# Turning v as float32r by way of a copy in HBM, with two small reorderings, in a fused attention and mixture-of-experts kernel

## The chip, the cores and the metric

The kernel runs on one core of a Trainium2 chip. Its engines are TensorE (PE for matmuls, PEld for the loads of their stationary operand), VectorE (DVE), ScalarE (ACT), GpSimd (POOL) and SyncE (SP), which here issues nearly all of the plain DMAs. Each engine works through its own queue in order, and semaphores order the engines among each other. The metric is the device time of one execution in microseconds (us); less is better.

## The reference

Four batches of q, k and v, each 5056 x 256 in float32, go through an attention over the channels, and its output goes through a mixture of eight experts of which each row takes one:

```python
qn = q / (np.linalg.norm(q, axis=1, keepdims=True) + 1e-06)
kn = k / (np.linalg.norm(k, axis=1, keepdims=True) + 1e-06)
s = kn.transpose(0, 2, 1) @ qn / tau            # 256 x 256 in each batch
a = softmax(s)
x = (v @ a).reshape(20224, 256)
logits = x @ w_gate + modality_bias[modality_id]
e_idx = argmax(logits); gate_w = softmax(logits)[e_idx]
out[rows of e] = gate_w * (np.maximum(x @ w1[e], 0) @ w2[e])   # w1[e]: 256 x 1024, w2[e]: 1024 x 256
```

## The kernel before, in words

**Numbers.** Most products are made of float32r matmuls: an operand is split into a high part (a copy that is rounded to float32r) and a low part (the rest), and three products (high by high, high by low, low by high) are summed in PSUM. The splits are a cast on ScalarE and a subtraction on DVE for each tile.

**Steps.** A batch is cut into ten steps of 512 rows (the last has 448), so there are 40 steps, g = 10 b + s. In a step, `va_pieces(b, s)` has two lists of pieces. The first one loads a tile of v (`load`, the DMA at L559) and turns it: `tr(h)` for the two halves of the channels, each with four transposes of 128 x 128 on TensorE (L576) into the PSUM tile `vtp`, then the high part `vh` on ScalarE (L580) and the low part `vl` on DVE (L582). The second list multiplies by the attention weights: `av(t)` (L596) makes the PSUM tile `xp` of 256 columns of x and 8 columns of logits, and ScalarE copies it out (L600). `route` then finds each row's expert and its place: maximum, exponentials on ScalarE (L611), one-hot rows `oh` (L619), a running count of them on DVE (`tensor_tensor_scan`, L627), three small matmuls `rp` (L632 to L634), positions, and the sum of the exponentials `sm` (L651) with its reciprocal as the gate's weight. Four indirect DMAs then scatter the rows of x to the scratch tensor `xs`, sorted by expert.

**Blocks.** A block is 512 rows (some 384) of one expert. Its rows are loaded from `xs` into a float32r tile `xr`, turned with the float32r identity (`tr_x`, L798) and split; then come eight hidden slices, `m1(j)` (L816, PSUM tag "h") with the activation on ScalarE (L819) and its low part on DVE (L820), and `m2(j)` (L834) into the output tiles; ScalarE scales them (L850) and an indirect DMA scatters them to the output. There are 40 blocks, with weights loaded for each (L758, L762) into buffers three deep and split (L779, L786).

**Next batch.** `kq_pieces(b + 1, s)` loads q and k (L291), squares and sums them (L333, L335) and adds their product to the 256 x 256 Gram matrix of the next batch (L344, L358, L362).

**At a batch's first step** `softmax_pieces(b)` turns the Gram matrix into weights: norms, two softmax pieces, `turn_weights` (transposes into the PSUM tile `atp`, L454, copied to `at` at L458) and `gate_weights`. For batches 1 to 3 the latter calls `gate_columns` for both halves, matmuls of `at` by the gate's matrix (L474) into the PSUM tile `gw`; their result becomes the last eight columns of the weights (L485, L488).

**The order of the work.** In each step the pieces of the block, of softmax, v and `av`, and of q and k are three streams, which `_interleave` mixes in proportion to their lengths; the second stream is written out at L955. From this order of the program a scheduler makes the queue of each engine; it may move a piece's instruction past others that aren't ready by its own model of the times. `order(ins, others)` lays down that an instruction stands behind others on its queue without a semaphore.

**PSUM.** `atp`, `gw`, `vtp` (from step 6 on), `xp`, `rp` and the turned x all have the tag "aux", which has two buffers of one bank each.

Of the kernel before, what the change touches and what calls it, by code (L numbers as in the profile page):

```python
# [34 lines left out]
def kernel(  # L35
# [349 lines left out]
    def softmax_pieces(b):  # L385
# [83 lines left out]
        def gate_columns(m, at):  # L469
            if m == 0:  # L470
                st["gw"] = ps2.tile([P, 512], F32, tag="aux", name=f"gw_{b}")
            gw = st["gw"]
            for jh in range(CH):
                nc.tensor.matmul(  # L474
                    gw[:, m * E : (m + 1) * E], at[:, jh, m * P : (m + 1) * P], small["wg"][:, jh, :],
                    start=(m == 0 and jh == 0), stop=jh == CH - 1, skip_group_check=True,
                )
# [33 lines left out]
    turned = {}  # L511
    routed = {}
# [32 lines left out]

    def va_pieces(b, s):
# [6 lines left out]
        def load():  # L553

            vt = p2.tile([P, TT, C], F32, tag="yo" if g % 2 == 1 and g < first_block else "v", name=f"v_{g}")
            if pp < P:
                z0 = pp // 32 * 32
                nc.vector.memset(vt[z0:], 0.0)
            nc.sync.dma_start(  # L559
                vt[:pp], v[b, t0 : t0 + pp * TT, :].rearrange("(p t) c -> p t c", t=TT)  # L560
            )
# [8 lines left out]
        def tr(h):  # L570
            if early and h == 1:
                tp = ps1.tile([P, 512], F32, tag="y1", name=f"vtp_{g}_{h}")
            else:
                tp = ps2.tile([P, 512], F32, tag="h" if early else "aux", name=f"vtp_{g}_{h}")
            for t in range(TT):
                nc.tensor.matmul(  # L576
                    tp[:, t * P : (t + 1) * P], st["v"][:, t, h * P : (h + 1) * P], ident,
                    is_transpose=True, start=t == 0, stop=True, skip_group_check=True,
                )
            cast[g] = nc.scalar.copy(st["vh"][:, h, :], tp).ins  # L580
            turned.setdefault(g, []).append(("act", cast[g]))
            ins = nc.vector.tensor_tensor(st["vl"][:, h, :], tp, st["vh"][:, h, :].bitcast(F32), ALU.subtract)  # L582
# [19 lines left out]
        def route():  # L602
# [24 lines left out]
            nc.vector.tensor_tensor_scan(rtf, keep, ohf, 0.0, ALU.mult, ALU.add)  # L627
# [23 lines left out]
            nc.vector.tensor_reduce(sm, ex, AX.X, ALU.add)  # L651
# [291 lines left out]
    for g in range(G):  # L943
# [11 lines left out]
        streams.append(soft[:-1] + turn[:1] + soft[-1:] + turn[1:] + va[g][1])  # L955
        if b + 1 < B:
            if b == 0 and s == 1:
                streams.append(list(kq_pieces(1, 2, lambda: routed[1] + turned[2], squares[2])))
            else:
                streams.append([f for i in (PLAN[s] if b == 0 else [s]) for f in kq_pieces(b + 1, i, routed[g - 1] + turned[g] if b == 0 and g > 0 else ())])  # L960
        _interleave(*streams)
# [94 lines left out]
```

## Time and profile before

| what | value |
|---|---|
| time, median of 3 runs | 1252.65 us (1251.12 to 1252.85) |
| the profiled execution's own time | 1244.78 us |
| its span, from the first to the last instruction | 1243.0 us |
| mean granted clock of TensorE | 0.998 |
| matmuls and other TensorE instructions | 8226 |
| moved by DMA | 210.82 MB, 170 GB/s in the mean |

The profile is of one execution. Busy times are given for each engine; a matmul's duration overlaps with its neighbours' since matmuls are pipelined, so the time that it takes from TensorE is read from the starts of two instructions that follow each other. A row of a timeline has the start, the duration, the engine, the line, the operation, the tiles (written <- read) and the count; in brackets stands how long the engine was idle before and what released it. A row of the waits has the engine and line that waited, what it waited for, the total, the number and the longest. The page gives the granted clock and the DMA share in 40 slices of the span, in tenths.

### The profile page before, as it was taken

The numbers are of one execution on the slowest core, as the hardware profiler recorded it, in microseconds if no ns is written. First come the engines' busy times: TensorE is split into PE (matmuls) and PEld (weight loads), VectorE is DVE, ScalarE is ACT, GpSimd is POOL, SyncE is SP. The second block draws the span as 40 slices with busy tenths as digits, with TensorE's granted clock in tenths as the row PEclk, the third lists the DMA queues.
The fourth block names the chain that finished last, engine by engine and source line by source line (L and its number), as shares of the span: only waits on it lengthen the run. The fifth ranks groups of instructions, "written<-read, shape, count | busy, mean of one in ns | idle before, by whom it ended". The sixth has DMA issues, their size and how long they took to land.

```text
span 1243.0 us, 23526 instructions
## 1 busy us (share of the span) xinstructions
PE 1222.3 (98%) x8226; PEld 1113.7 (90%) x8226; DVE 835.2 (67%) x2196; ACT 740.0 (60%) x1519; POOL 356.0 (29%) x344
## 2 busy tenths in 40 slices
PE   9989999999999999999999999999999999999997
PEld 8878898899999999988999999998899999999997
DVE  6689688777677776676766776665565665575552
ACT  6666677766666666665566665565555554545553
POOL 0052333222233333213332333322322233343221
PEclk9999999999999999999999999999999999999999
DMA  8959465455555555545555564434554444443420
GB/s 309 338 167 339 147 212 180 154 176 179 170 175 185 178 178 173 174 155 168 178 173 188 163 182 156 146 111 132 167 168 139 147 157 140 138 146 115 154 98 29
DMA packets 104177, 210.82 MB, mean 170 GB/s; under 512 B 11336, under 2 KB 52808, under 8 KB 104048
## 3 DMA queue, kind: packets, MB, share of 16 engines
q1 hardware_dynamic: 88304, 167.61, 42.7%
q0 software_dynamic: 15744, 41.61, 8.8%
q8 instruction: 66, 1.08, 0.4%
q14 instruction: 63, 0.52, 0.2%
HBM read 167.06 MB, written 43.43 MB: 169 GB/s over the span
## 4 chain that ended last, share of the span: by engine, by line
PE 87%; issue 7%; DMA 2%; DVE 2%; POOL 1%; ACT 1%; POOLq 0%; SPq 0%; DVEq 0%; ACTq 0%
PE y L834 31%; PE hp L816 31%; PE xp L596 10%; PE g L344 4%; PE g L358 4%; PE vtp L576 3%; PE g L362 2%; PE xtp L798 2%; POOL out_dram L515 1%; DMA k<-in_k_dram 1%; PE ns L395 1%; DMA w2r<-in_moe_w_dram 0%; PE gw L474 0%; DVE w1l L786 0%; DMA w1r<-in_moe_w_dram 0%
## 5 line engine op out<-in xcount | busy, mean ns | idle before, releaser
L515 POOL DMA_INDIRECT xs<-x,pi x160 | 178.9, 1118 | 694.4 <-ACT w1h L779 339.9
L834 PE MATMUL y<-w2h,hh 128*128 128x256 f32 x1264 | 355.5, 281 | 0.6 <-ACT yo L850 0.6
L834 PE MATMUL y<-w2l,hh 128*128 128x256 f32 x1264 | 353.4, 280 | 0.0
L834 PE MATMUL y<-w2h,hl 128*128 128x256 f32 x1264 | 352.6, 279 | 0.1
L820 DVE SCALAR_TENSOR_TENSOR hl<-hp,hh 128x512 fp32r<-128x512 f32 (+1 forms) x320 | 217.2, 679 | 65.7 <-ACT hh L819 62.5
L816 PE MATMUL hp<-xh,w1h 128*128 128x512 f32 (+1 forms) x640 | 255.9, 400 | 0.0
L834 PEld LDWEIGHTS y<-w2h,hh 128*128 128x128 f32 x1264 | 238.0, 188 | 14.8 <-ACT yo L850 1.3
L816 PE MATMUL hp<-xl,w1h 128*128 128x512 f32 (+1 forms) x640 | 251.0, 392 | 0.0
L816 PE MATMUL hp<-xh,w1l 128*128 128x512 f32 (+1 forms) x640 | 250.0, 391 | 0.0
L834 PEld LDWEIGHTS y<-w2l,hh 128*128 128x128 f32 x1264 | 238.6, 189 | 11.0
L819 ACT ACTIVATE hh<-hp 128x512 fp32r<-128x512 f32 (+1 forms) x320 | 190.3, 595 | 87.8 <-PE hp L816 75.8
L834 PEld LDWEIGHTS y<-w2h,hl 128*128 128x128 f32 x1264 | 237.4, 188 | 0.5 <-DVE hl L820 0.3
L515 POOL DMA_INDIRECT out_dram<-yo,xr x158 | 163.3, 1034 | 157.8 <-ACT yo L850 121.6
L786 DVE TENSOR_TENSOR w1l<-w1r,w1h 128x512 fp32r<-128x512 f32 x160 | 110.2, 689 | 133.2 <-ACT w1h L779 122.5
L779 ACT CAST w1h<-w1r 128x512 fp32r<-128x512 f32 x160 | 99.9, 624 | 136.7 <-PE hp L816 125.6
L816 PEld LDWEIGHTS hp<-xh,w1l 128*128 128x128 f32 x640 | 120.2, 188 | 25.4
L786 DVE TENSOR_TENSOR w2l<-w2r,w2h 128x512 fp32r<-128x512 f32 x160 | 111.3, 696 | 33.7 <-ACT w2h L779 31.5
L779 ACT CAST w2h<-w2r 128x512 fp32r<-128x512 f32 x160 | 100.9, 631 | 54.2 <-PE y L834 50.8
L816 PEld LDWEIGHTS hp<-xl,w1h 128*128 128x128 f32 x640 | 120.4, 188 | 14.2 <-DVE xl L804 0.4
L816 PEld LDWEIGHTS hp<-xh,w1h 128*128 128x128 f32 x640 | 120.2, 188 | 13.0
L596 PE MATMUL xp<-ah,vh 128*128 128x264 f32 x320 | 97.5, 305 | 3.8 <-DVE vl L582 1.7
L600 ACT COPY x<-xp 128x264 f32<-128x264 f32 x160 | 61.2, 383 | 52.3 <-PE xp L596 33.5
(154 smaller groups left out, 1773.2 us busy)
## 6 DMA issues: line engine op xcount, KB each, us to landing
w1r<-in_moe_w_dram SPq DMA_DIRECT2D x80, 512.0 KB
w2r<-in_moe_w_dram SPq DMA_DIRECT2D x80, 512.0 KB
xr<-xs SPq DMA_DIRECT2D x38, 516.0 KB
v<-in_v_dram SPq DMA_DIRECT2D x36, 512.0 KB
q<-in_q_dram SPq DMA_DIRECT2D x35, 512.0 KB
k<-in_k_dram SPq DMA_DIRECT2D x35, 512.0 KB
xs<-x,pi POOLq DMA_INDIRECT x160
out_dram<-yo,xr POOLq DMA_INDIRECT x158
```

The source lines that it names most:

```text
L344: nc.tensor.matmul(g[:, 0:C], st["k"][:pp, 2 * h + t, m * P : (m + 1) * P], st["q"][:pp, 2 * h + t, :], start=first, stop=last, skip_group ...
L358: nc.tensor.matmul(g, ks[:pp, t, m * P : (m + 1) * P], qs[:pp, t, :], start=first, stop=False, skip_group_check=True,)
L515: ins = nc.gpsimd.indirect_dma_start(out=dst, out_offset=bass.IndirectOffsetOnAxis(ap=idx, axis=0), in_=rows, in_offset=None, bounds_check ...
L576: nc.tensor.matmul(tp[:, t * P : (t + 1) * P], st["v"][:, t, h * P : (h + 1) * P], ident, is_transpose=True, start=t == 0, stop=True, skip ...
L596: nc.tensor.matmul(xp[:, 0:DE], a[:, h, t * P : (t + 1) * P], w[:, h, :], start=i == 0, stop=i == len(seq) - 1,)
L600: nc.scalar.copy(st["x"][:, t, :], xp[:, 0:DE])
L779: ins = nc.scalar.copy(hi, src).ins
L786: nc.vector.tensor_tensor(lo, src, hi.bitcast(F32), ALU.subtract)
L816: nc.tensor.matmul(hp[:, 0:rows], w[:, h, fs], x[:, h, 0:rows], start=i == 0, stop=i == len(seq) - 1)
L819: nc.scalar.activation(hh[:, 0:rows], hp[:, 0:rows], AF.Relu)
L820: nc.vector.scalar_tensor_tensor(hl[:, 0:rows], hp[:, 0:rows], 0.0, hh[:, 0:rows].bitcast(F32), ALU.max, ALU.subtract)
L834: ins = nc.tensor.matmul(y, a[:, tsl], w[:, j % 2, :], start=(j == 0 and i == 0 and t % 2 == 0), stop=(j == NJ - 1 and i == 2), skip_group ...
```

## The change

It has three parts.

- **v as float32r.** The tiles of v from step 12 on (`staged`) are first copied from v to a scratch tensor in HBM, `vs{g}`. The copy for step g + 4 is a piece in step g, in the middle of the step's last stream (the one of q and k in batches 0 to 2, the one of v and `av` in batch 3). `load` then reads the scratch instead of v into a tile that is declared float32r, and `tr` turns it with the float32r identity into a float32r PSUM tile, which the split reads as float32. Steps 0 to 11 are as before.
- **Gate's columns.** For batches 1 to 3, in the stream of the first step of the batch the whole turn of the next v stands ahead of `gate_weights`; before, its load alone did. In addition `order` puts each of the matmuls at L474 behind all of that step's transposes on TensorE's queue; `vturn[g]` is the list of the eight transposes of step g.
- **Exponentials' sum.** The sum of the exponentials on DVE (L651) is put behind the scan (L627) of the same step.

The diff:

```diff
--- before.py
+++ after.py
@@ -471,10 +471,12 @@
                 st["gw"] = ps2.tile([P, 512], F32, tag="aux", name=f"gw_{b}")
             gw = st["gw"]
             for jh in range(CH):
-                nc.tensor.matmul(
+                ins = nc.tensor.matmul(
                     gw[:, m * E : (m + 1) * E], at[:, jh, m * P : (m + 1) * P], small["wg"][:, jh, :],
                     start=(m == 0 and jh == 0), stop=jh == CH - 1, skip_group_check=True,
-                )
+                ).ins
+                if b > 0:
+                    order(ins, vturn[b * NS + 1])
 
         def gate_weights():
             ah, al = st["ah"], st["al"]
@@ -509,6 +511,7 @@
 
     cast = {}
     turned = {}
+    vturn = {}
     routed = {}
 
     def scatter(dst, idx, rows, groups, add, bound, why):
@@ -543,6 +546,20 @@
 
     first_block = LAG + START
 
+
+    staged = set(range(NS + 2, G))
+    vs = {
+        g: dram.tile([parts(g % NS) * TT, C], F32, name=f"vs{g}") for g in sorted(staged)
+    }
+
+    def stage(g):
+        b, s = divmod(g, NS)
+        n = parts(s) * TT
+        nc.sync.dma_start(
+            vs[g].rearrange("(p t) c -> p t c", t=TT),
+            v[b, s * STEP : s * STEP + n, :].rearrange("(p t) c -> p t c", t=TT),
+        )
+
     def va_pieces(b, s):
         pp = parts(s)
         g = b * NS + s
@@ -552,13 +569,13 @@
 
         def load():
 
-            vt = p2.tile([P, TT, C], F32, tag="yo" if g % 2 == 1 and g < first_block else "v", name=f"v_{g}")
+            dt = F32R if g in staged else F32
+            vt = p2.tile([P, TT, C], dt, tag="yo" if g % 2 == 1 and g < first_block else "v", name=f"v_{g}")
             if pp < P:
                 z0 = pp // 32 * 32
-                nc.vector.memset(vt[z0:], 0.0)
-            nc.sync.dma_start(
-                vt[:pp], v[b, t0 : t0 + pp * TT, :].rearrange("(p t) c -> p t c", t=TT)
-            )
+                nc.vector.memset(vt[z0:].bitcast(F32), 0.0)
+            src = vs[g] if g in staged else v[b, t0 : t0 + pp * TT, :]
+            nc.sync.dma_start(vt[:pp].bitcast(F32), src.rearrange("(p t) c -> p t c", t=TT))
             st["v"] = vt
             st["vh"] = p2.tile([P, CH, STEP], F32R, tag="vh", name=f"vh_{g}")
             st["vl"] = p2.tile([P, CH, STEP], F32R, tag="vl", name=f"vl_{g}")
@@ -571,15 +588,18 @@
             if early and h == 1:
                 tp = ps1.tile([P, 512], F32, tag="y1", name=f"vtp_{g}_{h}")
             else:
-                tp = ps2.tile([P, 512], F32, tag="h" if early else "aux", name=f"vtp_{g}_{h}")
+                dt = F32R if g in staged else F32
+                tp = ps2.tile([P, 512], dt, tag="h" if early else "aux", name=f"vtp_{g}_{h}")
             for t in range(TT):
-                nc.tensor.matmul(
-                    tp[:, t * P : (t + 1) * P], st["v"][:, t, h * P : (h + 1) * P], ident,
+                ins = nc.tensor.matmul(
+                    tp[:, t * P : (t + 1) * P], st["v"][:, t, h * P : (h + 1) * P], identr if g in staged else ident,
                     is_transpose=True, start=t == 0, stop=True, skip_group_check=True,
-                )
-            cast[g] = nc.scalar.copy(st["vh"][:, h, :], tp).ins
+                ).ins
+                vturn.setdefault(g, []).append(ins)
+            tf = tp.bitcast(F32) if g in staged else tp
+            cast[g] = nc.scalar.copy(st["vh"][:, h, :], tf).ins
             turned.setdefault(g, []).append(("act", cast[g]))
-            ins = nc.vector.tensor_tensor(st["vl"][:, h, :], tp, st["vh"][:, h, :].bitcast(F32), ALU.subtract)
+            ins = nc.vector.tensor_tensor(st["vl"][:, h, :], tf, st["vh"][:, h, :].bitcast(F32), ALU.subtract)
             if g == 0:
                 order(ins.ins, [i for _, i in weighted])
             turned[g].append(("dve", ins.ins))
@@ -624,7 +644,7 @@
             run_t = p2.tile([P, E, TT], BF16, tag="run", name=f"run_{g}")
             ohf = oh.rearrange("p e t -> p (e t)")
             rtf = run_t.rearrange("p e t -> p (e t)")
-            nc.vector.tensor_tensor_scan(rtf, keep, ohf, 0.0, ALU.mult, ALU.add)
+            scan = nc.vector.tensor_tensor_scan(rtf, keep, ohf, 0.0, ALU.mult, ALU.add).ins
             if early:
                 rp = ps1.tile([P, 512], F32, tag="y0", name=f"rp_{g}")
             else:
@@ -648,7 +668,8 @@
                 numbers = nc.vector.tensor_reduce(pi, pos.rearrange("p e t -> p t e"), AX.X, ALU.add)
             st["pi"] = pi
             sm = p2.tile([P, TT], F32, tag="sm", name=f"sm_{g}")
-            nc.vector.tensor_reduce(sm, ex, AX.X, ALU.add)
+
+            order(nc.vector.tensor_reduce(sm, ex, AX.X, ALU.add).ins, [scan])
             nc.vector.tensor_scalar(sm, sm, 1e-9, None, ALU.add)
             routed[g] = [
                 ("act", exps.ins),
@@ -952,12 +973,14 @@
         soft = list(softmax_pieces(b)) if s == 0 and b > 0 else []
         turn = va[g + 1][0] if g + 1 < G else []
 
-        streams.append(soft[:-1] + turn[:1] + soft[-1:] + turn[1:] + va[g][1])
+        streams.append(soft[:-1] + turn + soft[-1:] + va[g][1])
         if b + 1 < B:
             if b == 0 and s == 1:
                 streams.append(list(kq_pieces(1, 2, lambda: routed[1] + turned[2], squares[2])))
             else:
                 streams.append([f for i in (PLAN[s] if b == 0 else [s]) for f in kq_pieces(b + 1, i, routed[g - 1] + turned[g] if b == 0 and g > 0 else ())])
+        if g + 4 in staged:
+            streams[-1].insert(len(streams[-1]) // 2, lambda g=g: stage(g + 4))
         _interleave(*streams)
         run(squares.get(g + 1, []))
         if waiting and waiting[0][0] <= g + 1 - lag(g + 1):
```

## The prediction

> **What bounds the kernel now.** I read the page first, then the groups by line and shape, the waits of TensorE, and the timelines of the places that the change touches.
>
> ```profile
> span 1243.0 us, 23526 instructions
> PE 1222.3 (98%) x8226; PEld 1113.7 (90%) x8226; DVE 835.2 (67%) x2196; ACT 740.0 (60%) x1519; POOL 356.0 (29%) x344
> PEclk9999999999999999999999999999999999999999
> DMA  8959465455555555545555564434554444443420
> PE 87%; issue 7%; DMA 2%; DVE 2%; POOL 1%; ACT 1%; POOLq 0%; SPq 0%; DVEq 0%; ACTq 0%
> ```
>
> TensorE is busy for 98% of the span, at 0.9 or more of its clock in every slice, and it is 87% of the chain that ended last. The next engine, DVE, is at 67%, and the DMA engines are about half used in the steady part. So this is a kernel in which matmuls start one behind the other, and two things alone shorten it: less time between two starts on TensorE, or fewer gaps. The change tries both. How large the gaps are that it aims at, the first two of these waits say (total in us, times, longest; the third is needed below). The groups behind them show the two kinds of transpose that it exchanges (busy us, mean ns):
>
> ```profile
> PE gw L474 <- ACT at L458: 2.6, 3, 1.1
> PE rp L632 <- DVE sm L652: 1.4, 2, 0.8
> ACT sq_k L333 <- DMA k<-in_k_dram: 15.9, 14, 2.3
> ```
>
> ```profile
> L576 PE MATMUL vtp<-ident,v 128*128 128x128 f32 x320 | 43.8, 275 | 0.0
> L798 PE MATMUL xtp<-identr,xr 128*128 128x128 f32 x316 | 36.3, 238 | 0.2 <-issue 0.2
> ```
>
> The gaps in question are small, 2.6 and 1.4 us in 1243. The transposes are the larger matter. Their mean durations (275 and 238 ns) overlap with the neighbours and mustn't be subtracted; the time that a group takes from TensorE is the distance from its first start to the start of the next matmul. For v as plain float32, eight in a row, in the steady part:
>
> ```profile
> 653.22 1.04 PE L576 MATMUL vtp<-ident,v 128*128 128x128 f32 x8
> 654.01 0.47 PE L816 MATMUL hp<-xh,w1h 128*128 128x512 f32 x1
> 654.32 0.39 PE L816 MATMUL hp<-xl,w1h 128*128 128x512 f32 x1
> 654.54 0.40 PE L816 MATMUL hp<-xh,w1l 128*128 128x512 f32 x1
> ```
>
> and for the gathered rows x, which are float32r already and turned by the float32r identity, four in a row:
>
> ```profile
> 509.83 0.46 PE L798 MATMUL xtp<-identr,xr 128*128 128x128 f32 x4
> 510.12 0.36 PE L596 MATMUL xp<-ah,vh 128*128 128x264 f32 x1
> 510.32 0.29 PE L596 MATMUL xp<-al,vh 128*128 128x264 f32 x1
> 510.45 0.28 PE L596 MATMUL xp<-ah,vl 128*128 128x264 f32 x1
> ```
>
> Eight float32 transposes hold TensorE for 654.01 - 653.22 = 0.79 us, 99 ns each; four float32r ones for 0.29 us, 72 ns each. The matmul behind a group is late too: 0.31 against 0.22 us behind the float32 group, 0.20 against 0.13 us behind the float32r one, so about 0.08 us in either case.
>
> **The change part by part.**
>
> *Turning v as float32r.* Steps 12 to 39 are 28 steps, each with 8 transposes (320 in 40 steps, in the row of L576). A step's eight would take 2 x 0.29 = 0.58 us instead of 0.79, and the tail behind them stays. That is 0.21 us a step and 28 x 0.21 = 5.9 us; with the tail's 0.09 against 0.07 us it is 6.4. I take 6.2 us. The bound below: only the first four of a run go at the faster pace, and the other four at the old 99 ns; that is 0.79 - 0.29 - 0.40 = 0.10 us a step, 2.9 us. The bound above: in a run of eight a float32r transpose takes half of a float32 one, 0.40 us a step, 11 us. The row of four is the same instruction on the same shape, so I stay by it. The ScalarE copy and the DVE subtraction that follow read the same number of elements and aren't touched. What is late next, once these 0.22 us a step are gone? Nothing that a step of the steady part shows (busy us of PE, PEld, DVE, ACT and POOL, then the clock, the DMA share and GB/s):
>
> ```profile
> 600.00:630.00 30.00, 30.00 (x205) 27.35 (x204) 21.14 (x54) 19.31 (x40) 8.49 (x8) 1.00 0.55 174
> ```
>
> TensorE has no gap in these 30 us, and DVE and ScalarE have some 9 and 11 us free.
>
> The Trainium skill ("TensorE: Matmul & The Clock Gate", Part 1, "Wait — 56ns, not 53.3ns?") puts the distance of two starts at full clock at the columns divided by 2.4 GHz plus some 2.5 ns, 55.6 ns for 128 columns. By it the estimate would be eight in 0.44 us and a saving of 28 x 0.35 = 9.7 us. The row of 0.29 us for four doesn't agree, so the sum doesn't use it.
>
> *Staging.* There are 28 copies from v to scratch in HBM, one in each of steps 8 to 35, and the loads of v from step 12 on read the scratch instead. No trace of before has a copy from HBM to HBM. The nearest rows are the loads of v themselves and the full slices of the DMA row:
>
> ```profile
> v<-in_v_dram SPq DMA_DIRECT2D x36, 512.0 KB
> GB/s 309 338 167 339 147 212 180 154 176 179 170 175 185 178 178 173 174 155 168 178 173 188 163 182 156 146 111 132 167 168 139 147 157 140 138 146 115 154 98 29
> ```
>
> 512 KB at the 339 GB/s of the fullest slice is 1.5 us; if the read and the write count apart, 3.1 us of all DMA engines in a step of some 30 us, a tenth beside the half that is used. The copy is issued some three steps, about 85 us, before the load that waits for it, so this wait ends long before. SP issues one more instruction in a step, with nothing to wait for. I cost it at nothing; the cover is the idle half of the DMA engines. What it costs without that cover is the rival below.
>
> *Gate's columns behind the whole next turned v.* In batches 1 to 3 the second half of these matmuls stands right behind the copy of the weights just turned:
>
> ```profile
> 839.06 0.38 PE L454 MATMUL atp<-ident,ae 128*128 128x128 f32 x2
> ...
> 840.65 0.37 ACT L458 COPY at<-atp 128x256 f32<-128x256 f32 x1 [1.56 <-PE hp L816]
> ...
> 841.07 0.61 PE L474 MATMUL gw<-wg_sb,at 128*128 128x8 f32 x4 [1.05 <-ACT at L458]
> ...
> 841.54 0.97 PE L576 MATMUL vtp<-ident,v 128*128 128x128 f32 x4
> ```
>
> TensorE waits there for 1.05 us, with both groups of v's transposes behind it. The change puts all eight ahead. But the turned v (vtp), the turned weights (atp) and the gate's columns (gw) all have the tag "aux", which has two PSUM buffers. atp holds one of them until this same copy at L458 has read it. The first group of transposes can take the other; the second group must have atp's, so it waits for the copy that gw waited for, on the same in-order queue; gw, behind both, is then free at once. As I read it the wait changes its name, not its length: 0 is the value that I take. The ends are the whole gap gone (2.6 us, and what hangs on it, below) and the wait of gw for the first group's DVE subtraction on top (0.7 us three times, 2 us lost). No other work is queued for av of the new batch than before; the ScalarE and DVE copies of the 16 gate columns follow gw and come later by one group of transposes, with two block pieces between them and av.
>
> *The exponentials' sum behind the scan.* DVE runs its queue in order, and in one place the sum's wait for ScalarE holds the one-hot rows back, and with them TensorE:
>
> ```profile
> 97.78 0.18 DVE L651 TENSOR_REDUCE sm<-ex 128x4 f32<-128x32 f32 x1 [0.92 <-ACT w2h L779]
> 98.48 0.22 DVE L619 TENSOR_TENSOR oh<-val,vm 128x32 bf16<-128x32 f32 x1
> 98.76 0.19 PE L632 MATMUL rp<-oh,trim 128*128 128x32 bf16 x1 [0.61 <-DVE sm L652]
> ```
>
> With the sum behind the scan, oh and the scan no longer wait for it: 0.6 us of TensorE. In the other wait of this kind (0.8 us) the sum slipped into the pause between two dependent operations and the one-hot rows would have come then anyway. I take 0.6 us, between 0 and 1.4. The new order makes DVE wait at the sum instead, with one weight split behind it, as before.
>
> *Sum.* 6.2 + 0 + 0 + 0.6 = 6.8 us off the profiled execution, whose own time is 1244.78 us (1.78 around the span of 1243.0): 1238.0 us. The median of the runs shown, 1252.65 us, stands 7.9 us above that execution, and nothing in the trace says why; I carry the difference over and take 6.8 us off the median: **1245.8 us**.
>
> **The rivals.**
>
> *The gate's wait does vanish* (faster still). For it: if the second buffer is free by the time the transposes come, eight of them fill 0.6 to 0.8 of the 1.05 us. And more may hang on that gap. Behind the one at 840 us the clock fell:
>
> ```profile
> 838.00:841.60 3.60, 2.55 (x18) 2.00 (x17) 1.57 (x6) 1.81 (x4) 1.79 (x2) 1.00 0.38 95
> 841.60:845.00 3.40, 3.40 (x18) 3.40 (x18) 2.13 (x4) 1.36 (x4) 0.00 (x0) 0.51 0.84 280
> ```
>
> In these windows (the busy times of PE, PEld, DVE, ACT and POOL, then the granted clock) it is 0.51 over the 3.4 us that follow, which is 0.49 x 3.4 = 1.7 us lost. With 2.6 us of waits it makes 4.3 us, and 1241.5 us in all. Against it: the two other gaps of the same kind were followed by no drop, and the PSUM buffer above. The Trainium skill ("TensorE: Matmul & The Clock Gate", Part 1) lets the clock fall after an idle window of about 3.4 us; by that rule a gap of 1.05 us is too short, and taking it away would leave the 1.7 us. The trace agrees with the length of the slow stretch and shows the drop behind the gap all the same.
>
> *The copies stand in the way of k* (slower). The place is the load of k in batches 0 to 2:
>
> ```profile
> 616.23 0.35 SPq L291 DMA_DIRECT2D q<-in_q_dram  x1
> 617.03 0.57 SPq L291 DMA_DIRECT2D k<-in_k_dram  x1
> 622.59 0.63 ACT L333 ACTIVATE sq_k<-k 128x512 f32<-128x512 f32 x1 [2.27 <-DMA k<-in_k_dram]
> 623.65 0.57 ACT L819 ACTIVATE hh<-hp 128x512 fp32r<-128x512 f32 x1
> 624.47 0.68 DVE L820 SCALAR_TENSOR_TENSOR hl<-hp,hh 128x512 fp32r<-128x512 f32 x1
> 627.78 0.39 PE L816 MATMUL hp<-xh,w1h 128*128 128x512 f32 x1
> ```
>
> ScalarE already waits 2.27 us for k, and the hidden activations stand behind it on its queue. Their PSUM buffer is free at 624.47 + 0.68 = 625.15, and the matmuls that need it come at 627.78, so 2.6 us of delay are hidden. A copy that runs ahead of k costs it 1.5 to 3.1 us; from 2.6 us on, TensorE waits. At 3.1 us, 0.5 us are lost in each of the 22 steps 8 to 29 that have both a copy and a load of k: 11 us, and 1257 us. If the copy takes twice as long, it is 3.6 us a step, 79 us, and 1325 us. For it: k is late as it is. Against it: the copy is put in the middle of the pieces that begin with the loads of q and k, so it goes out behind them on SP's queue, and what comes next are weights, whose buffers are three deep.
>
> *Float32r is cheaper in a long run* (faster still). At the bound above, 11 us in place of 6.2, the time is 1241.0 us. For it: the last of a group carries a tail, and a run of eight has one where two runs of four have two. Against it: that tail is no larger than 0.08 us, 2 us in 28 steps, and only more than that brings the time there.
>
> *It doesn't do what it says* (same). The order of the instructions is made anew for the whole program, and a reordering that opens ten gaps of 0.6 us, such as the one above, gives the 6.2 us back: 1252 us. For it: TensorE has no slack and every gap counts. Against it: the step quoted above has no gap, and the change leaves its pieces nearly as they stand.
>
> **How the numbers follow.** The forecast (the transposes and the sum, with the gate's wait kept under another name; 1243.5 to 1248.5 us) gets 0.47. The gate's wait gone as well (1238.5 to 1243.5): 0.17. Transposes cheaper than the row of four (the same stretch): 0.08. Half of the gain given back (1248.5 to 1250): 0.06. All of it given back (1250 to 1255): 0.13. The copies in the way (above 1255): 0.09. What a measurement of this kernel can tell from no change is about 0.2%, 2.5 us, so "same" is 1250.1 to 1255.2. Faster: 0.78; same: 0.13; slower: 0.09. A range of 1239 to 1254 leaves out the tail of the large gain and the slower case.
>
> **What would show it.** The step's eight transposes at L576 should take near 0.58 us from first start to the next matmul in steps 12 to 39 and stay at 0.79 before. The wait of gw for the copy at L458 should be gone, and one of vtp for the same copy should stand in its place, three times; if neither is there, the first rival holds. The wait of rp for sm should be gone. The waits of ScalarE for k show the copies: 12 us or so in all if they are hidden. The forecast is wrong if float32r transposes in a run of eight don't keep the pace of four, or if TensorE shows new waits of more than 4 us in all.

## The result, and the profile after

The changed kernel takes 1273.19 us in the median of 4 runs (1266.24 to 1278.99); the kernel before, on the same chip, 1251.88 us (1248.80 to 1252.85). The ratio is 1.0171, with a 95% interval of 1.0148 to 1.0194: slower by 1.7%, where 1245.8 us, 0.5% faster, was forecast, and outside the range of 1239 to 1254. On one other chip of this study the changed kernel is the faster one (1228.55 against 1232.72 us), and the explanation has to cover that too; all that follows in this section is from the first chip.

The profiled execution took 1272.06 us. Its page, with the rows that answer to those of before:

```profile
span 1270.1 us, 23547 instructions
PE 1227.4 (97%) x8226; PEld 1116.0 (88%) x8226; DVE 838.7 (66%) x2196; ACT 742.1 (58%) x1519; POOL 363.2 (29%) x344
PEclk9989899999999999999999999999899999999999
DMA  8959897455555555545555554434444444433420
GB/s 311 329 193 380 296 331 262 142 167 181 184 172 182 176 178 183 169 142 179 181 188 182 176 179 134 133 132 133 133 133 133 134 151 138 142 126 125 161 96 28
PE 81%; issue 10%; DVE 3%; ACT 2%; DMA 2%; POOL 1%; another core or an unknown queue 0%; POOLq 0%; SPq 0%; ACTq 0%
```

The engines do the same work, but TensorE's part of the chain that ended last falls from 87% to 81%, and the clock has three slices with an 8, one of them some seven tenths into the span. So there are gaps on TensorE that weren't there, and half-clock stretches behind them. The waits of TensorE (total in us, times, longest) name the gaps; the sixth line is one of ScalarE, and the last is the first one's counterpart from before:

```profile
PE xp L616 <- DVE vl L602: 17.1, 6, 3.7
PE y L855 <- issue: 3.9, 7, 1.1
PE xp L616 <- ACT x L620: 3.3, 1, 3.3
PE xp L616 <- issue: 2.6, 2, 2.3
PE vtp L594 <- ACT at L458: 1.6, 2, 1.3
ACT sq_k L333 <- DMA k<-in_k_dram: 14.5, 15, 1.8
PE xp L596 <- DVE vl L582: 1.7, 2, 1.1
```

17.1 us are lost where the product by the attention weights (`xp`) waits for the low part of the turned v; it was 1.7 before. The four largest of these waits, 13.4 us, fall into steps 31 to 34, and the gap of 2.3 us in step 35 stands under "issue"; all five are in batch 3. One of them in the timeline (start, duration, engine, line, operation, count, idle time before and releaser; GpSimd's scatters included):

```profile
901.87 1.02 POOL L518 DMA_INDIRECT xs<-x,pi  x1 [0.30 <-issue]
...
902.14 0.80 PE L594 MATMUL vtp<-identr,v 128*128 128x128 f32 x8
902.38 0.84 ACT L871 ACTIVATE yo<-y,xr 128x256 f32<-128x256 f32 x2 [0.56 <-PE y L855]
902.77 0.47 PE L837 MATMUL hp<-xh,w1h 128*128 128x512 f32 x1
...
903.20 1.00 POOL L518 DMA_INDIRECT out_dram<-yo,xr  x1 [0.30 <-ACT yo L871]
...
904.00 0.40 PE L837 MATMUL hp<-xh,w1l 128*128 128x512 f32 x1
904.50 0.98 POOL L518 DMA_INDIRECT out_dram<-yo,xr  x1 [0.30 <-issue]
905.25 0.47 ACT L871 ACTIVATE yo<-y,xr 128x256 f32<-128x256 f32 x1 [2.03 <-PE hp L837]
906.00 0.98 POOL L518 DMA_INDIRECT out_dram<-yo,xr  x1 [0.52 <-issue]
906.69 0.59 ACT L600 CAST vh<-vtp 128x512 fp32r<-128x512 f32 x1 [0.97 <-remote]
907.31 0.69 DVE L602 TENSOR_TENSOR vl<-vtp,vh 128x512 fp32r<-128x512 f32 x1 [4.67 <-issue]
908.06 0.59 PE L616 MATMUL xp<-ah,vh 128*128 128x264 f32 x1 [3.66 <-DVE vl L602]
```

and the same place in the kernel before:

```profile
891.81 0.98 POOL L515 DMA_INDIRECT xs<-x,pi  x1 [0.31 <-issue]
...
894.46 1.03 PE L576 MATMUL vtp<-ident,v 128*128 128x128 f32 x8
...
895.42 0.99 POOL L515 DMA_INDIRECT out_dram<-yo,xr  x1 [2.63 <-ACT yo L850]
896.10 1.10 ACT L580 CAST vh<-vtp 128x512 fp32r<-128x512 f32 x2
896.75 1.29 DVE L582 TENSOR_TENSOR vl<-vtp,vh 128x512 fp32r<-128x512 f32 x2 [1.14 <-ACT vh L580]
...
898.11 0.28 PE L596 MATMUL xp<-ah,vh 128*128 128x264 f32 x1
```

Two things come together here. First, `xp` now stands right behind the first hidden slice (`hp`): the order on TensorE is 12 matmuls of `y`, 8 `vtp`, 6 `hp`, 6 `xp`, 12 `y`, and in steps 31 to 35 of before it is 12 `y`, 8 `vtp`, 6 `hp`, 12 `y`, 6 `xp`. It needs one of the two PSUM buffers of the tag "aux", and `vtp` holds them until DVE has read the turned v for the low part. Second, that split comes late without any work ahead of it: the eight transposes are over by 902.94 and the `y` matmuls in front of them earlier still, ScalarE is idle from 903.22 on, and yet its next scaling of `y` begins at 905.25 and its cast of the first half of v at 906.69. ScalarE was told late that TensorE was done.

The new order does a third thing: it moves GpSimd's scatters onto the transposes. In steps 32 to 35 of before, the last scatter of x starts 2.64 us ahead of the first transpose and the first scatter of the output 1.0 us behind it, and the cast of v begins 1.65 to 1.71 us behind it. In steps 31 to 35 of the changed kernel the last scatter of x starts 0.03 to 0.27 us ahead, and the cast begins 3.2 to 4.6 us behind.

Behind the gap TensorE runs at half its clock. The windows (busy times of PE, PEld, DVE, ACT and POOL, then the granted clock, DMA share and GB/s):

```profile
903.00:907.60 4.60, 1.40 (x6) 0.79 (x5) 0.29 (x1) 1.28 (x3) 2.96 (x3) 0.90 0.49 193
907.60:911.00 3.40, 2.94 (x13) 2.94 (x14) 2.39 (x4) 2.24 (x5) 0.98 (x1) 0.50 0.57 186
```

The starts of the eight transposes in steps 31 to 36, in the two traces, give the bill:

| kernel | transposes of v start at (us) | five steps |
|---|---|---|
| before | 866.27, 894.46, 921.62, 948.74, 975.86, 1003.02 | 136.75 us |
| changed | 871.04, 902.14, 935.36, 967.50, 998.29, 1027.68 | 156.64 us |

These five steps alone lose 19.9 us; TensorE's idle time ahead of `xp` is 15.7 us of it, and three of the five gaps have a half-clock stretch behind them. In the step from 1055.68 to 1082.64, which has the old order, the changed kernel takes 26.96 us where before takes 27.12 (1030.14 to 1057.26), so there it does gain. The steps up to 8 lose another 10.4 us in these two traces (the first `xp` of step 9 starts at 205.25 us against 194.90), and steps 9 to 29 win 5.4 back. What makes the early loss isn't shown: a later trace with the same order on TensorE ("no output scatters" below) has it at 3.8 us.

### The profile page after: what moved, and what is told of

The parts are those of the page before. It is cut to its first block, busy times and chain, and to the rows that moved or that the text cites. A ratio compares the mean times of both kernels' runs of the same rounds, so it can differ in the third digit from the quotient of the medians.

```text
span 1270.1 us, 23547 instructions
## 1 busy us (share of the span) xinstructions
PE 1227.4 (97%) x8226; PEld 1116.0 (88%) x8226; DVE 838.7 (66%) x2196; ACT 742.1 (58%) x1519; POOL 363.2 (29%) x344
## 4 chain that ended last, share of the span: by engine, by line
PE 81%; issue 10%; DVE 3%; ACT 2%; DMA 2%; POOL 1%; another core or an unknown queue 0%; POOLq 0%; SPq 0%; ACTq 0%
PE y L855 30%; PE hp L837 29%; PE xp L616 9%; PE g L344 3%; PE g L358 3%; PE vtp L594 2%; PE g L362 2%; PE xtp L819 2%; POOL out_dram L518 1%; DMA k<-in_k_dram 1%; PE ns L395 1%; DVE vl L602 0%; DVE acc L335 0%; ACT yo L871 0%; DMA xs<-x,pi 0%
## 5 line engine op out<-in xcount | busy, mean ns | idle before, releaser
L518 POOL DMA_INDIRECT out_dram<-yo,xr x158 | 171.4, 1085 | 155.9 <-ACT yo L871 116.7
L616 PE MATMUL xp<-ah,vh 128*128 128x264 f32 x320 | 98.8, 309 | 23.2 <-DVE vl L602 17.1
L602 DVE TENSOR_TENSOR vl<-vtp,vh 128x512 fp32r<-128x512 f32 x80 | 54.7, 689 | 58.6 <-issue 36.4
```

What stands on the lines that cost most here:

```text
L518: ins = nc.gpsimd.indirect_dma_start(out=dst, out_offset=bass.IndirectOffsetOnAxis(ap=idx, axis=0), in_=rows, in_offset=None, bounds_check ...
L602: ins = nc.vector.tensor_tensor(st["vl"][:, h, :], tf, st["vh"][:, h, :].bitcast(F32), ALU.subtract)
L616: nc.tensor.matmul(xp[:, 0:DE], a[:, h, t * P : (t + 1) * P], w[:, h, :], start=i == 0, stop=i == len(seq) - 1,)
```

## The experiments

The kernels of one group ran on one chip, beside the kernel before. "Late" counts the completions of TensorE for which the next recorded update of their semaphore came more than 0.6 us behind the start of the matmul, out of some 1,185 in a run. The traces of some chips lack up to a tenth of these records, and a missing one counts as late, so it is a rough count; with missing ones left out, 65 to 114 remain on the chips with many (called late chips here) and at most 1 on the others.

| group, before (us) | kernel | median us | ratio, 95% interval | late |
|---|---|---|---|---|
| first chip, 1251.88 | changed | 1273.19 | 1.0171 (1.0148 to 1.0194) | 167 (before: 163) |
| 1, 1232.66 | empty piece | 1234.01 | 1.0008 (0.9999 to 1.0018) | 0 |
| | copies outside | 1232.01 | 0.9984 (0.9974 to 0.9994) | 1 |
| | copies paced | 1231.60 | 0.9995 (0.9983 to 1.0006) | 2 |
| | transposes only | 1230.63 | 0.9978 (0.9968 to 0.9987) | 4 |
| 2, 1232.72 | changed | 1228.55 | 0.9962 (0.9948 to 0.9976) | 1 |
| | gate's columns only | 1233.25 | 1.0006 (0.9996 to 1.0015) | 0 |
| | sum only | 1233.42 | 1.0003 (0.9993 to 1.0012) | 1 |
| 3, 1246.21 | changed | 1264.22 | 1.0138 (1.0084 to 1.0192) | 155 |
| | empty piece | 1265.16 | 1.0146 (1.0111 to 1.0181) | 181 |
| | copies outside | 1244.11 | 0.9996 (0.9974 to 1.0019) | 157 |
| 4, 1244.66 | copies paced | 1243.93 | 0.9997 (0.9983 to 1.0012) | 154 |
| | transposes only | 1241.40 | 0.9980 (0.9968 to 0.9993) | 172 |
| 5, 1251.64 | changed | 1273.28 | 1.0162 (1.0134 to 1.0191) | 178 |
| | no output scatters | 1255.53 | 1.0036 (1.0013 to 1.0059) | 162 |
| | scatters behind xp | 1260.09 | 1.0073 (1.0043 to 1.0104) | 168 |

**The order alone.** A copy is a piece, and a piece in the middle of the stream of v and `av` (steps 30 to 35, where batch 3 has no stream of q and k) shifts where `_interleave` puts the others. An empty piece in the kernel before does only that:

```diff
+        if b == B - 1 and g + 4 < G:
+            streams[-1].insert(len(streams[-1]) // 2, lambda: None)
         _interleave(*streams)
```

> The kernel before, with an empty piece in the middle of the stream of v and av in steps 30 to 35, where the change puts its copy; no copy, no float32r, nothing else. Theory A (the piece takes a slot in the mix of streams, so xp comes right behind the turned v and m1 instead of behind m2, and waits for the PSUM buffer in steps 31 to 35): five gaps of 2.5 to 3.8 us at xp with slow-clock stretches behind them, 16 to 23 us above before, 1267 to 1275 us. Theory B (the copies' traffic makes the loss): as before, 1250 to 1254 us, and no gap above 1.5 us at xp in the last batch.

Measured: 1.0008, no loss; theory A's number was missed. The trace shows why. TensorE's order in steps 31 to 35 is that of the changed kernel, and in steps 32 to 35 GpSimd's scatters stand where they do there, but the split follows the transposes at once. Rows of its timeline:

```profile
912.13 1.03 PE L576 MATMUL vtp<-ident,v 128*128 128x128 f32 x8
...
913.12 1.10 ACT L580 CAST vh<-vtp 128x512 fp32r<-128x512 f32 x2
...
913.77 1.29 DVE L582 TENSOR_TENSOR vl<-vtp,vh 128x512 fp32r<-128x512 f32 x2 [1.14 <-ACT vh L580]
...
914.16 0.40 PE L816 MATMUL hp<-xh,w1l 128*128 128x512 f32 x1
...
914.51 0.39 PE L596 MATMUL xp<-ah,vh 128*128 128x264 f32 x1
```

The cast begins 1.0 us behind the first transpose, where it was 4.5 us above, and `xp` starts 0.35 us behind the last `hp`, without a wait. But this chip had run the kernel before in 1232.66 us, not 1251.88, so the miss could be the theory's or the chip's.

**The copies elsewhere, and the transposes alone.** Two edits take the copy out of the streams; the second also holds it back on SP's queue, and a third kernel has that and neither of the two small parts:

```diff
-            streams[-1].insert(len(streams[-1]) // 2, lambda g=g: stage(g + 4))
+            stage(g + 4)
```

```diff
+        order(ins.ins, [vload[g - 4]])
```

> The changed kernel, with the copy issued ahead of the mixing of the streams instead of as a piece of one; all else as changed. Theory A: the gaps at xp in the last batch go, 18 to 23 us below the changed kernel, 1249 to 1255 us; what the early burst of copies costs (gaps between 60 and 200 us) stays. Theory B: as the changed kernel, 1266 to 1279 us.

> As the run before, and each copy is also put behind the load of v four steps before its own on SP's queue, so that the copies go out one in a step instead of 28 between 62 and 200 us. If the burst costs the 8 us by which the gaps of the first 200 us grew: 1241 to 1247 us. If it costs nothing: as the run before it. In both cases the eight transposes of a step take 0.58 to 0.65 us.

> As the paced run, with gate's columns and the exponentials' sum where they were before: only v's turn as float32r by the paced copy. If the transposes are worth the 6 us of the prediction and nothing else moved: 1244 to 1248 us. The difference to the paced run is what the two small reorderings are worth: 0 to 2 us by the prediction, up to 5 us if the gate's wait goes with its slow-clock stretch.

Measured: 0.9984, 0.9995 and 0.9978. The times expected were for a chip like the first, and without late completions there are no gaps to remove, so theories A and B aren't told apart here. A gain of the transposes is there, 2.0 us in the last, and pacing the copies brings nothing. The kernel of the last has the order of before on TensorE, so its gain is the transposes' alone, and it is less than half of the 6.2 us that were forecast.

Its trace shows one place where the gain may go, step 10 (ScalarE's wait for q, then TensorE's for the one-hot rows):

```profile
202.22 0.63 ACT L333 ACTIVATE sq_q<-q 128x512 f32<-128x512 f32 x1 [3.02 <-DMA q<-in_q_dram]
211.34 0.19 PE L652 MATMUL rp<-oh,trim 112*128 112x32 bf16 x1 [1.52 <-DVE oh L639]
```

The granted clock is halved for 3.41 us behind it, and from the first `xp` of step 9 to that of step 11 it is 67.9 us; in the kernel with the sum alone, which has no copies (group 2), the two waits are 2.02 and 0.51 us, the clock stays, and it is 65.5 us. With the copies outside the streams it is 68.9 us, but paced 65.8 and in the changed kernel of group 2 63.6. These are single executions; whether a copy makes q late stays open.

**The changed kernel on another chip.**

> The changed kernel itself, unaltered, beside the kernel before on one chip. In the trace of the changed kernel TensorE's semaphore updates reached ScalarE late at the gaps (the first half of v was turned by 902.7 us, its cast began at 906.69, the second half's at 908.14); in the run with the empty piece, on another chip, the same order had no gap. Theory C (the order exposes TensorE to late updates, which come on one chip and not on another): if before is near 1232 us here, the changed kernel is near 1230 to 1234 us, without a gap over 1 us at xp in steps 31 to 35; if before is near 1252 us, it is near 1270 us again. Theory D (the copies' burst together with the order makes the loss on any chip): 15 to 22 us above before wherever it runs.

Measured: 1228.55 against 1232.72 us, 0.9962: faster, by 4.2 us. One wait of `xp` for `vl` is left in its trace, of 1.1 us at 88.6 us, and none of those in steps 31 to 35. Theory C fits; D, a loss that the changed kernel carries everywhere, falls. In the same group the two small parts ran alone, each as in the diff of the change:

> The kernel before with the second part of the change alone: gate's columns behind the whole next turned v. By the prediction 0 (the wait of gw for the copy becomes one of the turned v for the same copy), 1 us either way; if the wait vanishes, 2.6 us and up to 4.3 us less.

> The kernel before with the third part alone: the exponentials' sum behind the scan. By the prediction 0.6 us less, 0 to 1.4; the wait of rp for sm is gone.

Measured: 1.0006 and 1.0003, nothing. The kernel with the sum alone, whose gate is the old one, has no wait of `gw` on this chip, so the first part had nothing to win here.

**The same three on one chip.** With theory C the empty piece should cost as much as the whole change, but only where completions come late.

> The changed kernel once more, beside the two runs that follow, on one chip. If the kernel before takes near 1250 us here (a chip like the first): theory C (the order of steps 31 to 35 puts xp right behind the turned v, and late updates of TensorE's completions turn that into gaps) expects 1266 to 1279 us again, with five waits of xp for the subtraction of v at L602, 2.5 to 3.8 us each. If the kernel before takes near 1232 us: theory C expects 0.3 to 0.4% faster again and no more than one such wait. Theory D (the first result was an accident of that one day and not of the chip) expects 0.3 to 0.4% faster on either.

> The kernel before, with an empty piece in the middle of the stream of v and av in steps 30 to 35, which gives TensorE the order of the changed kernel there and nothing else of it. If the kernel before takes near 1250 us here: theory C expects 10 to 25 us more than it, from the same five gaps at xp (L596). If the order isn't what makes them (theory E: it is the copies' traffic or the float32r transposes), as before within 0.2%. If the kernel before takes near 1232 us: both expect no difference, as in the first run of this kernel.

> The changed kernel with each copy issued ahead of the step's streams instead of as a piece within one, so that the order of TensorE in steps 31 to 35 is that of the kernel before. If the kernel before takes near 1250 us here: theory C expects 4 to 7 us less than it (the transposes' 4.3 us and the sum), theory E as slow as the changed kernel. If the kernel before takes near 1232 us: 0.1 to 0.4% faster than it by both.

This chip ran before in 1246.21 us. The changed kernel lost 1.38% and the empty piece 1.46%, and with the copies outside the streams the loss was gone, at 0.9996. So the order of steps 31 to 35 by itself makes a loss as large as the whole change's, with no copy, no float32r and nothing else of the change in it; theory E falls. The size of the gain with the copies outside (4 to 7 us) was missed: 2.1 us, within its interval of no change. The same stretch of the empty piece's kernel on the two chips, as windows (columns as above), first the chip of group 1, then that of group 3:

```profile
860.00:1030.00 170.00, 170.00 (x1170) 154.82 (x1170) 102.16 (x277) 90.10 (x187) 51.71 (x52) 1.00 0.51 157
```

```profile
860.00:1030.00 170.00, 156.47 (x1021) 141.66 (x1020) 90.75 (x251) 80.39 (x165) 47.63 (x48) 0.95 0.41 137
```

One and the same program fills TensorE in 170.0 of 170 us on one chip and in 156.5 on the other, at 0.95 of the clock. Two windows of the latter show how one gap is paid for:

```profile
927.80:931.20 3.40, 0.02 (x1) 0.00 (x0) 0.69 (x1) 0.66 (x2) 2.79 (x3) 0.87 0.34 139
931.20:934.60 3.40, 3.36 (x15) 3.36 (x16) 1.98 (x3) 1.97 (x4) 0.08 (x1) 0.50 0.68 202
```

3.4 us of nothing, then 3.4 us at half the clock, 1.7 us more. GpSimd is busy through the gap, for 2.79 of 3.40 us, and idle behind it.

**Do the early copies cost anything?** All 28 copies go out between 62 and 197 us, not one in a step. The view of that line in the changed kernel (instruction, count, shortest, median and longest duration in ns, first and last start):

```profile
L558 SPq DMA_DIRECT2D vs<-in_v_dram x28: 494/533/607, 62.1 to 196.9; - x28
```

> The changed kernel with the copies outside the streams, and each copy ordered on SP's queue behind the load of v eight steps before its own load, so that none is issued in the first steps. If the kernel before takes near 1246 us here: theory F (the copies that the scheduler moved to 62 to 197 us cost time in the early steps) expects 1240 to 1243 us, that is 2 to 5 us better than with the copies unpaced, and TensorE's gap near 70 us back at 1.3 us or so; theory G (the early gaps come from the late updates alone, wherever the copies are) expects as before within 0.3%. If the kernel before takes near 1232 us: 0.1 to 0.4% faster than it by both.

> The same without the changes to gate's columns and to the exponentials' sum: float32r transposes of v through paced copies alone. If the kernel before takes near 1246 us here: 4.3 us less than it (28 steps by the measured 0.15 us) where nothing gives it back, with the waits of gw for L458 and of rp for the sum present as before; within 1.5 us of the paced kernel, since the two small parts showed no effect alone. If the kernel before takes near 1232 us: 0.2 to 0.4% faster, as in the first run of this kernel.

(The edit is that of the paced kernel above: each copy goes behind the load of v four steps before its own, not eight.) Measured: 0.9997 paced, against 0.9996 unpaced on another late chip, and the gap of TensorE near 73 us stayed at 3.3 us. Theory F falls: when the copies go out makes no difference that shows. Whether they are free altogether isn't shown, with step 10 as above: on this chip too, the kernel with the transposes alone has a wait of 3.3 us for q there and one of 1.85 us for the one-hot rows. The transposes alone gained 3.3 us (0.9980). That the paced kernel with the two small parts is 2.5 us behind it was not expected (1.5 us was the bound); on the chip of group 1 it was 1.0 us. The intervals overlap on both chips, and alone the two parts cost nothing, so whether they cost anything together with the transposes stays open.

**What holds the completions up.** In all traces of late chips, 93 to 99% of the late completions, counted as in the table, are of matmuls that started within or just behind (0.3 us) an indirect DMA's issue on GpSimd, as some 30% of all of them do; of the completions that fall due in such a stretch 38 to 46% are late, of the others 1 to 2%. With missing records left out, TensorE's completions come up to 3.3 to 5.0 us behind the matmul's start in these traces, while of ScalarE's none and of DVE's at most one in a trace comes more than 0.3 us behind its instruction's end: what is held up is TensorE's. In steps 31 to 35 GpSimd issues eight in a row, four for the rows of x and four for the block's output. One kernel leaves the latter out in steps 30 to 35, and one makes them wait for the step's first `xp`:

```diff
+            if cur[0] in range(30, 36):
+                return
             ins = scatter(
                 out, st["xr"].bitcast(I32)[:, t, D + 1 : D + 2], yo, ["y"], ["y"], T - 1,
```

```diff
+            if cur[0] in range(30, 36):
+                held.append(put)
+                return
+            ins = put()
...
+            while held:
+                after(held.pop(0)(), [last])
```

(`put` is the scatter, `last` the last matmul of `xp` in `av`, `cur` the step.)

> The changed kernel as it is, as the measure for the two that follow on the same chip. Where the kernel before takes 1240 to 1253 us and TensorE's completions come late: 1.3 to 1.8% slower than before, with gaps of 2.1 to 3.8 us ahead of xp (L616) in steps 31 to 35. Where before takes near 1232 us: 0.3 to 0.4% faster.

> The changed kernel without the scatters of the blocks' output rows in steps 30 to 35 (so these rows of the output aren't written); the order on TensorE is that of the changed kernel. Where completions come late: theory P (TensorE's completions are held up while GpSimd issues indirect DMAs, and it issues four of these scatters just then) expects the five gaps at xp gone or under 1 us and a time 15 to 25 us under the changed kernel's, at or below before. Theory L (completions are late at that place whatever GpSimd does) expects the gaps and the time of the changed kernel. Where they aren't late, both expect the changed kernel's time within 0.3%.

> The changed kernel with all its scatters, but in steps 30 to 35 the scatters of the output rows wait for the last matmul of that step's first xp. Where completions come late: theory P expects no gap of over 1 us ahead of the first xp and 10 to 25 us under the changed kernel (new late completions behind xp, with 12 matmuls of y next, may give some back); theory L expects the gaps and the time of the changed kernel. Where they aren't late, both expect the changed kernel's time within 0.3%.

Measured on this late chip: changed 1273.28, without the scatters 1255.53 and with the scatters moved 1260.09 us, so 17.8 and 13.2 us are back (the last in the median of runs that spread from 1252.57 to 1268.42); the order on TensorE is the same in all three. Since moving the scatters helps as well, it isn't only the missing output traffic. The timeline of the kernel without them, at the place of the first one above:

```profile
891.90 1.02 POOL L518 DMA_INDIRECT xs<-x,pi  x1 [0.30 <-issue]
...
892.16 0.80 PE L595 MATMUL vtp<-identr,v 128*128 128x128 f32 x8
...
893.84 0.47 ACT L872 ACTIVATE yo<-y,xr 128x256 f32<-128x256 f32 x1 [0.65 <-PE vtp L595]
...
894.21 1.06 ACT L601 CAST vh<-vtp 128x512 fp32r<-128x512 f32 x2
894.82 1.29 DVE L603 TENSOR_TENSOR vl<-vtp,vh 128x512 fp32r<-128x512 f32 x2 [2.15 <-ACT vh L601]
...
895.56 0.39 PE L617 MATMUL xp<-ah,vh 128*128 128x264 f32 x1 [1.14 <-DVE vl L603]
```

ScalarE hears of TensorE again at 893.84, 0.9 us after the last scatter of x ended at 892.92, and the gap is 1.14 us in place of 3.66. Theory P stands in kind; theory L, by which nothing should have moved, falls. In size P promised too much: four of the five gaps are left with 1.1 to 1.4 us, behind the scatters of x, and 0.36% over before was measured where "at or below" was expected. More than that is lost outside the edit's reach: in step 36, where the output's scatters are back, the profiled execution takes 33.6 us against 27.1 before. The order on TensorE there is the old one, but the last scatter of x starts 0.28 us ahead of the transposes, the cast comes 4.5 us behind them, and `y` waits 2.55 us. The 12 matmuls of `y` are no cover there, since they wait themselves, for ScalarE's scaling; so where the scatters fall matters too, and not only what stands in between. P's figure for the moved scatters (10 to 25 us) was met. Why a scatter's issue holds the completions up, and on some chips only, is not shown; what was shown is that taking it away or moving it shortens the gaps.

## Why the prediction was wrong

**The step that failed is "Staging".** It costed the 28 copies at nothing with the idle half of the DMA engines as cover. As a transfer they cost little, if anything: ScalarE's waits for k are 14.5 us against 15.9, the DMA row is at 4 to 5 tenths in the steady part, and paced or not the time is the same, though the copies went out in the first 197 us and not one in a step. But the step priced a piece as a DMA alone. `_interleave` mixes streams in proportion to their lengths, so a piece in the middle of the stream of v and `av` moves every piece behind it; in batch 3 that put `xp` in front of the 12 matmuls of `y` that had stood between it and the turn of v. These 12 were part of the cover of the split; the same order also put the scatters of x onto the transposes, and the cast came 3.2 to 4.6 us behind them instead of 1.7. Which of the two weighs more was not separated. An empty piece, which transfers nothing, costs the same 1.4% on a late chip. In most of steps 11 to 28 the order on TensorE differs as well, in 22 places of a step, without such gaps (steps 11 to 29 take 583.4 us against 585.9).

**The rival that came true had the wrong price.** "It doesn't do what it says" spoke of a reordering that opens gaps, allowed ten of 0.6 us to give 6.2 us back, and held against it that the change leaves its pieces nearly as they stand. In steps 31 to 35 it doesn't. Five gaps of 2.3 to 3.7 us and the half clock behind three of them made 19.9 us. That completions can come late could have been read from before: there the copy at L458 began at 840.65 for transposes that started at 839.06, 1.6 us, with GpSimd's scatters running. I put that gap down to the wait for `gw` as such and didn't ask why the copy itself was late. A delay as long as those of the changed kernel stands in before once: the second half of v turned from 562.5 us on is cast 5.0 us later, at 567.49.

**The transposes were right in kind, too large in size.** Eight now hold TensorE from 902.14 to 902.77, 0.63 us (0.636 in the median of the steady steps), not 0.58: 79.5 ns each where the row of four gave 72. That is 0.154 us a step and 28 x 0.154 = 4.3 us in place of 6.2. The Trainium skill ("TensorE: Matmul & The Clock Gate", Part 2, "Back-to-back issue gap") puts a sustained stream of weight loads and matmuls at some 81 ns for 128 columns; the trace agrees with that, and not with the 55.6 ns of the section that the prediction weighed, which that page gives for a matmul by itself.

**Gate's columns went as read in two places of three.** The wait of `gw` is gone, and one of `vtp` for the same copy at L458 stands in its place, 1.6 us against 2.6, though twice and not three times. The first rival, that it vanishes, holds for one of the three places: the gap of 1.05 us at 841 us, and the half clock behind it, have no counterpart in the changed trace. Alone, on the chip of group 2, the part is worth nothing that can be measured; on a late chip it did not run alone.

**The exponentials' sum** lost its wait of `rp` for `sm` in the changed trace; its 0.6 us can't be told from nothing. **The copies in the way of k** and **float32r cheaper in a long run** are out by the waits for k and by the 79.5 ns.

**The sum as it should have been**: on a chip without late completions 4.3 us off; on a late chip some 19 us more for the order, as the empty piece alone has it. That the changed kernel gained 4.2 us in group 2 is in part luck: the transposes alone gained 2.0 us on the like chip of group 1, though their steady steps are shorter by the 0.15 us each. On late chips too the gain doesn't show in full: 2.1 us with the copies outside, 3.3 us with the transposes alone. Step 10 is one place where it goes in the traces; the rest stays open. The prediction had one chip's trace, and that chip was a late one.

## What to carry to other kernels

A piece put into a mixed stream is priced by what it moves, not only by what it does: compare the order of each engine's queue before and after, and for each pair that has come closer together ask what covered the distance, and what other engines now do at the same time. Read the real delay between the end of a matmul and the start of the instruction that waits for it, in the places where GpSimd scatters, rather than from the best step; a pair that is just in time by a model has no margin. The transposes through paced copies alone were faster on the one chip of each kind on which they ran (0.9978, and 0.9980 on a late one), so they are the safer version of this change.

## What the runs showed of the hardware

Chips differ: the kernel before takes 1232.7 us on two of them and 1244.7 to 1251.9 on the others. On the first two, half of TensorE's completions are recorded within 0.3 us of the matmul's start and, by the table's count, at most 4 of some 1,185 later than 0.6 us; on the others 154 to 181 are, nearly all while GpSimd issues indirect DMAs. What sets these chips apart isn't shown.

The granted clock fell behind gaps shorter than I expected. In the kernel with the empty piece on the late chip, a gap of 1.96 us that ended at 898.99 was followed by this window, in which the clock is halved from 899.6 on:

```profile
899.00:902.40 3.40, 3.40 (x18) 3.40 (x19) 1.29 (x2) 1.58 (x3) 1.20 (x2) 0.59 0.73 243
```

A gap of 2.29 us that ended at 1002.84 in the changed kernel was followed by no drop. In the clock's own record the half-clock stretches last 3.41 or 6.83 us (but for the one at the end of a run), and their starts lie whole multiples of 3.41 us apart, in each trace that has several. The Trainium skill ("TensorE: Matmul & The Clock Gate", Part 1, "What's actually happening") has the clock fall after at least one idle window of some 3.4 us and lets that window run freely; the slow stretch's length agrees, and so does the fixed grid, but the length of the gap that brings it doesn't.
